# Eight small slots of 80, 64 and 48 tokens in an expert layer, both matrices stationary, and a written order on SyncE's queue

## The chip, the core and the metric

One core of a Trainium2 chip runs the whole program. The metric is the device time of one execution in microseconds (us). Engines are named as in the profile: PE (TensorE matmuls), PEld (TensorE weight loads), DVE (VectorE), ACT (ScalarE), POOL (GpSimd), SP (SyncE, which here only issues DMAs and loads registers). L809 is line 809 of the kernel before.

## The reference

Three layers in a row over 2304 tokens of 512 features. The change is in the last one, a mixture of eight experts of which each token takes two:

```python
def _moe2_ref(x, w_gate, w_noise, noise, w1, w2):
    logits = x @ w_gate
    noise_scale = np.log1p(np.exp(x @ w_noise))
    noisy_logits = logits + noise_scale * noise
    top2 = np.argpartition(-noisy_logits, 2, axis=1)[:, :2]
    ...
    for e in range(E):                      # 8 experts, D = 512, F = 1024
        for k in range(2):
            mask = top2[:, k] == e
            h = np.maximum(x[mask] @ w1[e], 0.0)
            out[mask] += top2_w[mask, k, None] * (h @ w2[e])
```

With the inputs of this case the experts 0 to 7 get 148, 573, 208, 22, 292, 1614, 1033 and 718 tokens (counted with the reference). Cut into blocks of 128, the last block of each holds 20, 61, 80, 22, 36, 78, 9 and 78 tokens.

## The kernel before

The first two layers, the gate and the sorting of tokens by expert take the first 450 us, and the change leaves them alone but for a few small DVE operations on eight numbers in the schedule. Then comes the expert stage. Tokens of one expert are dealt into **main blocks** of 128; the program has room for 36 of them, expert after expert (here 5, 6, 0, 7, 2, 1, 4). A last block of up to 64 tokens may go into one of five **small slots** of 64; the first five such experts by number get one (here 0, 1, 3, 4 and 6). `SEQ` is the fixed list of the 41 pieces: after the main blocks 8, 14, 20, 26 and 32 stands a small slot. What falls outside would run in a tail that is skipped here.

Values are split in fp16 high and low parts, and each product is three matmuls (high by high, low by high, high by low). A main block's first layer (`e1`, L809) is 24 matmuls with the block's tokens stationary and 512 weight columns moving, into the PSUM tile `ph`; ACT takes the relu (L816), DVE the low part (L817), and 16 DVE transposes of 32x32 squares (L830) bring `hr` to `ht`. The second layer (`e2`, L873) is again 24 matmuls of 512 columns into `py`; ACT scales it into `y` (L885) and POOL adds it into the output by an indirect DMA (L886). A small slot's `e1_small` (L843) has the weights stationary and 64 tokens moving, 96 matmuls, so that its output needs no transpose; its `e2_small` (L859) is 24 matmuls of 512 columns with 64 tokens stationary.

One step `t` of the loop puts on PE `e1(SEQ[t])` and then `e2(SEQ[t-3])`. What the other engines do is issued in the same loop:

- **Main weights.** `weights(i, half)` (L773) loads 2 MB, conditional on a flag: a block whose expert is that of the block before it moves nothing. Two halves of a buffer alternate by expert. W1(i+2), the first layer's weights, is issued after `e1(i)` and W2(j+2) after `e2(j)`. Before each W1, SP loads three registers. The first main blocks of the experts, whose loads are real, are here blocks 0, 13, 21, 22, 28, 30 and 34 of `SEQ`'s main blocks before the change (expert 3 has a small slot alone).
- **Small weights.** `weights_small` (L760) loads a slot's weights in four pieces of 1 MB, S1 high, S1 low, S2 high, S2 low, into a place of its own that all slots share. The four go out at the ends of the steps that stand in the loop below, counted from the slot before.
- **Tokens.** `prep` copies the block's token list (L782), gathers the tokens into `xr` by an indirect DMA on POOL's queue (L785), and issues on SP the DMA transpose `xt<-xr` (L792), all in the step six ahead of use.

```python
        for half, a, later in ((0, 0, 1), (0, 1, 2), (1, 0, 4), (1, 1, 5)):
            k = PARTS.get(t - later)
            if k is not None:
                weights_small(k, half, a)
        while preps and SEQ.index(preps[0]) <= t + AHEAD + 1 and (preps[0] < NBA or t >= PB):
            prep(preps.pop(0))
```

All SP issues are one in-order stream, and their DMAs one queue (q1 in the profile); POOL's are another (q0). `issue_after` and `LAST[...]` fix the order on an engine where they are used; transposes of later blocks are placed by the scheduler.

Of the kernel before, what the change touches and what calls it, by code (L numbers as in the profile page):

```python
# [22 lines left out]
P = 128  # L23
# [12 lines left out]
NSMALL = 5  # L36
NMAIN = 36
# [49 lines left out]
def body(ctx, tc, ins, out):  # L87
# [528 lines left out]
    def small(ni, nb, new, tt, ts, red):  # L616
        rest = ts(ni, 127, None, ALU.bitwise_and, dt=I32)
        few = ts(rest, 64.0, None, ALU.is_lt)
        some = tt([NE], few, ts(nb, 0.0, None, ALU.is_gt), ALU.mult)
        a, b = iota[:, None, :NE].to_broadcast([P, NE, NE]), iota[:, :NE, None].to_broadcast([P, NE, NE])  # L620
        less = tt([NE, NE], a, b, ALU.is_lt, F16)
        turn = red(tt([NE, NE], less, some[:, None, :].to_broadcast([P, NE, NE]), ALU.mult, F16))
        POS["turn"] = turn
        POS["small"] = tt([NE], some, ts(turn, float(NSMALL), None, ALU.is_lt), ALU.mult)
        POS["at"] = new(NE)
        nc.vector.scalar_tensor_tensor(out=POS["at"], in0=iota[:, :NE], scalar=float(NB), in1=nb, op0=ALU.mult, op1=ALU.add)
# [99 lines left out]
    SEQ = [i for m in range(NMAIN) for i in ((m, NBLK + m // 6 - 1) if m > 5 and m % 6 == 2 else (m,))]  # L726
    TI, XE, HT, PY, PT, REG, LIST, E = {}, {}, {}, {}, {}, {}, {}, {}
# [28 lines left out]
    def weights_small(i, half, a):  # L756
        with behind("sync"):
            if half + a == 0:
                WR[i] = nc.sync.value_load(entry(i, 2), min_val=0, max_val=NE - 1)
            w = nc.sync.dma_start(out=AR[half][:, 16384 + a * 4096:20480 + a * 4096],  # L760
                                  in_=wsc[ds(WR[i], 1), :, half, a].rearrange("o p f -> p (o f)"))
        (W1, W2)[half].setdefault(i, []).append(w)

    def weights(i, half):


        with behind("sync"):
            if half == 0:
# [5 lines left out]
                                  in_=wsc[ds(e, 1), :, half].rearrange("o p a f -> p (o a f)"), cond=(c == 1))  # L774
        (W1, W2)[half][i] = [w]

    def prep(i):
        ep, tab, at = E["ep"], LIST["a" if i < NBA else "b"][1], SEQ.index(i) if i in SEQ else i
# [9 lines left out]

        xt = E["ep2"].tile([P, 8, P], F16, name="xt2", bufs=2) if at > 5 and at % 3 == 0 else \
            ep.tile([P, 8, P], F16, name="xt", bufs=4)  # L790
        with behind("sync") if i < NBA else ExitStack():
            LAST["sync"] = nc.sync.dma_start_transpose(out=xt, in_=xr)  # L792
        TI[i], XE[i] = ti, xt
# [39 lines left out]
    def e1_small(i):  # L833
        xt, m = XE.pop(i), 0
        ph = E[bank(i)].tile([P, 512], F32, tag="ph", name="ph", bufs=2)
        ht = E["ep2"].tile([P, 2 * F2], F16, tag="ht", name="ht", bufs=5)
        M1[i] = []
        for f in range(8):
            with after() if f == 0 else ExitStack():
                for k in range(KC):  # L840
                    for a, b in ((0, 0), (1, 0), (0, 1)):
                        w = 16384 + b * 4096 + k * 1024 + f * 128
                        M1[i].append(nc.tensor.matmul(ph[:, f * HALF:(f + 1) * HALF], lhsT=AR[0][:, w:w + 128],  # L843
                                                      rhs=xt[:, a * 4 + k, :HALF], start=k + a + b == 0, stop=k == KC - 1 and b == 1))
# [34 lines left out]
    def combine(i):  # L879
# [3 lines left out]
        y, m = E["ep2"].tile([P, DM], F32, name="y", bufs=3), HALF if i >= NBLK else P  # L883
# [155 lines left out]
    LAG, AHEAD = 3, 5  # L1039
# [28 lines left out]
    for t in range(2, len(SEQ) + LAG):  # L1068
# [25 lines left out]
        for half, a, later in ((0, 0, 1), (0, 1, 2), (1, 0, 4), (1, 1, 5)):  # L1094
            k = PARTS.get(t - later)
            if k is not None:
                weights_small(k, half, a)
        while preps and SEQ.index(preps[0]) <= t + AHEAD + 1 and (preps[0] < NBA or t >= PB):
            prep(preps.pop(0))
            if preps and preps[0] == NBA + 2 and t == PB:  # L1100
                break
    weight_deps()
    with tc.If(nc.values_load(LIST["more"], min_val=0, max_val=1) > 0):  # L1103
        for i in range(NMAIN, NBLK):
# [3 lines left out]
            prep(i)  # L1108
            REG[i] = nc.tensor.value_load(entry(i, 1), min_val=0, max_val=1)
# [29 lines left out]
```

## Time and profile before

| | |
|---|---|
| runs | 889.49, 884.94, 885.11 us; median 885.11 us |
| profiled execution | 888.15 us; its span, first to last instruction, 886.4 us |
| mean granted TensorE clock | 0.988 |
| busy, share of the span | PE 97%, DVE 70%, PEld 50%, ACT 43%, POOL 32% |
| expert stage | from 450 us to the end at 886.4 us |

Times in the views below are counted from the span's first instruction. The span is 1.75 us shorter than the execution's own time.

### The profile page before, as it was taken

What the parts mean: (1) busy time and instruction counts of PE and PEld (TensorE: products, weight loads), DVE (VectorE), ACT (ScalarE), POOL (GpSimd) and SP (SyncE); (2) the same over time, 40 slices, a digit from 0 to 9 for tenths busy, and PEclk for the clock granted to TensorE, in tenths of its full rate; (3) what the DMA queues carried; (4) which work ended last, traced back from release to release, by engine and by line L of the source; (5) the groups of instructions that cost most, each with busy time, mean ns of one, the idle gap of its engine ahead of it and who ended that gap; (6) DMA issues with size and microseconds to landing.
All of it is one profiled execution on the core that took longest, in us unless ns stands there. A gap on an engine that the chain in (4) does not pass through costs nothing. (4 is left out here: it accounts for less than half of the span.)

```text
span 886.4 us, 19836 instructions
## 1 busy us (share of the span) xinstructions
PE 855.5 (97%) x6826; PEld 445.5 (50%) x6826; DVE 621.6 (70%) x1299; ACT 384.8 (43%) x599; POOL 287.6 (32%) x276
## 2 busy tenths in 40 slices
PE   6799999999999999999999999999999999989995
PEld 6455555555555555555544444445445445434542
DVE  5999978686786777554459785775885886758552
ACT  3989767676665786574421121221212111211110
POOL 3876224242612412422305323222233222312212
PEclk9899999999999999999999999999999999989998
DMA  9977599899799898962776986787559998697442
GB/s 335 383 292 210 189 269 326 286 308 327 248 328 327 278 314 311 317 218 52 225 185 132 179 162 147 215 203 194 155 125 301 215 236 228 165 296 186 166 120 40
DMA packets 143908, 203.72 MB, mean 230 GB/s; under 512 B 79872, under 2 KB 90368, under 8 KB 139456
## 3 DMA queue, kind: packets, MB, share of 16 engines
q1 hardware_dynamic: 133632, 181.34, 65.7%
q0 software_dynamic: 10176, 21.05, 12.3%
q8 instruction: 63, 1.03, 0.5%
q14 instruction: 37, 0.30, 0.1%
HBM read 245.67 MB, written 53.55 MB: 338 GB/s over the span
## 5 line engine op out<-in xcount | busy, mean ns | idle before, releaser
L830 DVE STREAM_TRANSPOSE ht<-hr 32x256 f32<-32x256 f32 x528 | 230.1, 436 | 10.2 <-DVE hr L817 0.5
L321 PE MATMUL pg<-x,wi 128*128 128x384 f16 x1152 | 203.8, 327 | 1.4 <-POOL x L310 0.8
L809 PE MATMUL ph<-w,xt 128*128 x864 | 195.3, 383 | 5.2 <-DMA w<-wsc 4.5
L363 PE MATMUL p<-w,g 128*128 128x512 f16 x864 | 199.7, 379 | 0.0
L873 PE MATMUL py<-w,ht 128*128 x864 | 192.1, 379 | 0.2 <-DMA w<-wsc 0.2
L886 POOL DMA_INDIRECT out_dram<-y,ti x41 | 64.3, 1568 | 278.0 <-ACT y L885 225.1
L321 PEld LDWEIGHTS <-wi 128*128 128x128 f16 x1152 | 110.8, 98 | 82.2 <-issue 3.2
L809 PEld LDWEIGHTS <-xt 128*128 128x128 f16 x864 | 84.8, 99 | 110.2 <-issue 11.5
L873 PEld LDWEIGHTS <-ht 128*128 128x128 f16 x864 | 84.2, 98 | 101.2 <-DMA w<-wsc 0.6
L363 PEld LDWEIGHTS <-g 128*128 128x128 f16 x864 | 83.4, 98 | 91.9 <-issue 0.2
L817 DVE SCALAR_TENSOR_TENSOR hr<-ph,hr 128x512 f16<-128x512 f32 x72 | 52.4, 728 | 107.4 <-ACT hr L816 106.5
L816 ACT ACTIVATE hr<-ph 128x512 f16<-128x512 f32 x72 | 52.6, 732 | 141.1 <-PE ph L809 141.1
L885 ACT ACTIVATE y<-py,ti 128x512 f32<-128x512 f32 (+1 forms) x41 | 28.2, 687 | 187.2 <-PE py L873 163.8
L400 DVE SCALAR_TENSOR_TENSOR w<-w 128x1024 f16<-128x1024 f32 x64 | 90.9, 1446 | 16.1 <-ACT w L396 15.7
L332 ACT ACTIVATE r<-pg 128x384 f32<-128x384 f32 x96 | 46.9, 488 | 102.3 <-PE pg L321 97.9
L342 DVE SCALAR_TENSOR_TENSOR r<-a,r 128x768 f32<-128x768 f32 x48 | 49.1, 1022 | 56.6 <-ACT a L338 49.2
L350 POOL TENSOR_TENSOR g<-r,g 128x768 f16<-128x768 f32 x27 | 46.9, 1737 | 95.6 <-ACT g L142 51.2
L595 POOL DMA_INDIRECT table<-tb,pos x36 | 44.4, 1233 | 75.1 <-DVE scb L649 23.3
L396 ACT ACTIVATE w<-w 128x1024 f16<-128x1024 f32 x64 | 65.6, 1054 | 1.4 <-DMA w<-in_moe_w_dram 1.4
L785 POOL DMA_INDIRECT xr<-X,ti x41 | 43.3, 1055 | 23.4 <-DMA xt<-xr 11.6
L333 ACT ACTIVATE a<-pg 128x384 f32<-128x384 f32 x96 | 46.6, 485 | 0.0
L338 ACT ACTIVATE a<-a 128x768 f32<-128x768 f32 x48 | 40.6, 845 | 1.5
(152 smaller groups left out, 698.2 us busy)
## 6 DMA issues: line engine op xcount, KB each, us to landing
w<-wsc SPq DMA_DIRECT2D x68, 2048.0 KB
w<-in_moe_w_dram SPq DMA_DIRECT2D x64, 512.0 KB
wsc<-w SPq DMA_DIRECT2D x64, 512.0 KB
w<-wsc SPq DMA_DIRECT2D x20, 1024.0 KB
kv<-in_kv_dram SPq DMA_DIRECT2D x18, 512.0 KB
qk<-in_qk_dram SPq DMA_DIRECT2D x18, 512.0 KB
w<-in_moe_w_out_dram SPq DMA_DIRECT2D x8, 1024.0 KB
w<-in_moe_w_in_dram SPq DMA_DIRECT2D x7, 1024.0 KB
```

What stands on the lines that cost most here:

```text
L321: nc.tensor.matmul(pg, lhsT=wi[:, a, k, f * P:(f + 1) * P], rhs=x[:, b, k, :], start=n == 0, stop=n == 11)
L332: LAST["relu"] = nc.scalar.activation(PG["r", i][:, j], pg, AF.Relu, scale=S_G / SX)
L342: nc.vector.scalar_tensor_tensor(out=r, in0=PG.pop(("a", i)), scalar=S_G, in1=r, op0=ALU.mult, op1=ALU.add)
L363: LAST["p2"] = nc.tensor.matmul(PG[t, j], lhsT=g[:, a, f % 2, j * P:(j + 1) * P], rhs=wo[b][:, f, :], start=f == 0 and a + b == 0, stop=f ...
L396: nc.scalar.activation(h[:, 0], WL[n], AF.Copy, scale=(S_W1, S_W2)[(n // 4) % 2])
L400: nc.vector.scalar_tensor_tensor(out=h[:, 1], in0=t, scalar=(S_W1, S_W2)[(n // 4) % 2], in1=h[:, 0], op0=ALU.mult, op1=ALU.subtract)
L809: M1[i].append(nc.tensor.matmul(ph, lhsT=xt[:, a * 4 + k, :], rhs=AR[0][:, ds(r * 8192 + (b * 4096 + k * 1024 + n * 512), 512)], start=m = ...
L816: LAST["act"] = nc.scalar.activation(hi, ph, AF.Relu)
L817: nc.vector.scalar_tensor_tensor(out=lo, in0=ph, scalar=0.0, in1=hi, op0=ALU.max, op1=ALU.subtract)
L830: nc.vector.transpose(dst[32 * f:32 * f + 32, :, t], src[32 * t:32 * t + 32, :, f])
L873: M2[i].append(nc.tensor.matmul(py, lhsT=ht[:, c, :, a], rhs=AR[1][:, ds(r * 8192 + (b * 4096 + c * 512), 512)], start=len(M2[i]) == 0, st ...
L886: LAST["pool"] = nc.gpsimd.indirect_dma_start(out=out[:, :], out_offset=bass.IndirectOffsetOnAxis(ap=ti[:m, 1:2], axis=0), in_=y[:m, :], i ...
```

## The change

There are eight small slots instead of five, of 80, 80, 80, 64, 48, 48, 48 and 48 tokens. Experts are ranked by the size of their last block, the largest first, and a last block goes into the slot of its rank if it fits. With this case's inputs all eight fit (80, 78, 78, 61, 36, 22, 20 and 9 tokens), one of them exactly. The program has room for 33 main blocks, so `SEQ` still has 41 pieces; the slots stand after the main blocks 7, 10, 13, ..., 28, which is every fourth piece from `SEQ[8]` on. The first main blocks of experts are now 0, 12, 20, 21, 26, 27 and 31.

`e1_small` (L868 after the change) moves as many tokens as the slot has, into two `ph` tiles with a relu and a low part each. `e2_small` (L887) has the weights stationary too: 96 matmuls of the slot's tokens, and 8 or 12 DVE transposes out of PSUM into `y` (L895). ACT scales `y` in place. S2's pieces go out a step earlier than before. A transpose on SP is no longer issued with its gather but in the step four ahead of use (`turn`), and every SP issue of the loop is tied to the one before it.

```diff
--- before.py
+++ after.py
@@ -33,8 +33,9 @@
-NSMALL = 5
-NMAIN = 36
+CAPS = (80, 80, 80, 64, 48, 48, 48, 48)
+NSMALL = len(CAPS)
+NMAIN = 33
...
-        few = ts(rest, 64.0, None, ALU.is_lt)
+        few = ts(rest, float(max(CAPS)), None, ALU.is_lt)
...
+        key = new(NE)
+        nc.vector.scalar_tensor_tensor(out=key, in0=rest, scalar=8.0, in1=iota[:, :NE], op0=ALU.mult, op1=ALU.add)
+        more = tt([NE, NE], a, b, ALU.is_gt, F16)
+        turn = red(tt([NE, NE], more, some[:, None, :].to_broadcast([P, NE, NE]), ALU.mult, F16))
...
-        POS["small"] = tt([NE], some, ts(turn, float(NSMALL), None, ALU.is_lt), ALU.mult)
+        POS["small"] = tt([NE], some, tt([NE], cap, rest, ALU.is_gt), ALU.mult)
...
-    SEQ = [i for m in range(NMAIN) for i in ((m, NBLK + m // 6 - 1) if m > 5 and m % 6 == 2 else (m,))]
+    AT = [7 + 3 * n for n in range(NSMALL)]
+    SEQ = [i for m in range(NMAIN) for i in ((m, NBLK + AT.index(m)) if m in AT else (m,))]
...
                 WR[i] = nc.sync.value_load(entry(i, 2), min_val=0, max_val=NE - 1)
             w = nc.sync.dma_start(out=AR[half][:, 16384 + a * 4096:20480 + a * 4096],
                                   in_=wsc[ds(WR[i], 1), :, half, a].rearrange("o p f -> p (o f)"))
+        LAST["sync"] = w
         (W1, W2)[half].setdefault(i, []).append(w)
...
+        TI[i], XR[i] = ti, xr
+        if i < NBA:
+            turn(i)
+
+    def turn(i):
+        ep, xr, at = E["ep"], XR.pop(i), SEQ.index(i) if i in SEQ else i
         xt = E["ep2"].tile([P, 8, P], F16, name="xt2", bufs=2) if at > 5 and at % 3 == 0 else \
             ep.tile([P, 8, P], F16, name="xt", bufs=4)
-        with behind("sync") if i < NBA else ExitStack():
+        with behind("sync"):
             LAST["sync"] = nc.sync.dma_start_transpose(out=xt, in_=xr)
-        TI[i], XE[i] = ti, xt
+        XE[i] = xt
...
     def e1_small(i):
-        xt, m = XE.pop(i), 0
-        ph = E[bank(i)].tile([P, 512], F32, tag="ph", name="ph", bufs=2)
+        xt, m, rows = XE.pop(i), 0, CAPS[i - NBLK]
         ht = E["ep2"].tile([P, 2 * F2], F16, tag="ht", name="ht", bufs=5)
+        hs = HT[i] = ht[:, :16 * rows].rearrange("p (a c t) -> p a c t", a=2, c=8)
         M1[i] = []
-        for f in range(8):
-            with after() if f == 0 else ExitStack():
-                for k in range(KC):
+        for n in range(2):
+            ph = E[bank(i)].tile([P, 512], F32, tag="ph", name="ph", bufs=2)
+            for f in range(4):
+                with after() if f == 0 else ExitStack():
+                    for k in range(KC):
+                        for a, b in ((0, 0), (1, 0), (0, 1)):
+                            w = 16384 + b * 4096 + k * 1024 + (n * 4 + f) * 128
+                            M1[i].append(nc.tensor.matmul(ph[:, f * rows:(f + 1) * rows], lhsT=AR[0][:, w:w + 128],
+                                                          rhs=xt[:, a * 4 + k, :rows], start=k + a + b == 0,
+                                                          stop=k == KC - 1 and b == 1))
+            LAST["pe"] = M1[i][-1]
+            hi, lo = (hs[:, a, n * 4:n * 4 + 4].rearrange("p c t -> p (c t)") for a in range(2))
+            LAST["act"] = nc.scalar.activation(hi, ph[:, :4 * rows], AF.Relu)
+            nc.vector.scalar_tensor_tensor(out=lo, in0=ph[:, :4 * rows], scalar=0.0, in1=hi, op0=ALU.max, op1=ALU.subtract)
+
+    def e2_small(i):
+        hs, rows = HT.pop(i), CAPS[i - NBLK]
+        wide = -(-rows // 32) * 32
+        full = hs.rearrange("p a c t -> p a (c t)")
+        py = E[bank(i)].tile([P, 4, P], F32, tag="py", name="py", bufs=2)
+        M2[i] = []
+        for g in range(4):
+            with after() if g == 0 else ExitStack():
+                for c in range(8):
                     for a, b in ((0, 0), (1, 0), (0, 1)):
-                        w = 16384 + b * 4096 + k * 1024 + f * 128
-                        M1[i].append(nc.tensor.matmul(ph[:, f * HALF:(f + 1) * HALF], lhsT=AR[0][:, w:w + 128],
-                                                      rhs=xt[:, a * 4 + k, :HALF], start=k + a + b == 0, stop=k == KC - 1 and b == 1))
-        LAST["pe"] = M1[i][-1]
-        hi, lo = (ht[:, a * 512:(a + 1) * 512] for a in range(2))
-        LAST["act"] = nc.scalar.activation(hi, ph, AF.Relu)
-        nc.vector.scalar_tensor_tensor(out=lo, in0=ph, scalar=0.0, in1=hi, op0=ALU.max, op1=ALU.subtract)
-        HT[i] = ht[:, :1024].rearrange("p (a c t) -> p c t a", a=2, c=8)
-
-    def e2_small(i):
-        ht = HT.pop(i)
-        py = E[bank(i)].tile([P, DM], F32, tag="py", name="py", bufs=2)
-        M2[i] = []
-        for c in range(8):
-            with after() if c == 0 else ExitStack():
-                for a, b in ((0, 0), (1, 0), (0, 1)):
-                    w = 16384 + b * 4096 + c * 512
-                    M2[i].append(nc.tensor.matmul(py[:HALF], lhsT=ht[:, c, :, a], rhs=AR[1][:, w:w + 512],
-                                                  start=len(M2[i]) == 0, stop=len(M2[i]) == 23))
+                        w, n = 16384 + b * 4096 + c * 512 + g * 128, wide if c + a + b == 0 else rows
+                        M2[i].append(nc.tensor.matmul(py[:, g, :n], lhsT=AR[1][:, w:w + 128],
+                                                      rhs=full[:, a, c * rows:c * rows + n],
+                                                      start=c + a + b == 0, stop=c == 7 and b == 1))
         LAST["pe"] = M2[i][-1]
-        PY[i] = py
+        y = PY[i] = E["ep2"].tile([P, DM], F32, name="y", bufs=3)
+        v = y.rearrange("p (g f) -> p g f", g=4)
+        for f in range(4):
+            for t in range(wide // 32):
+                nc.vector.transpose(v[32 * t:32 * t + 32, :, 32 * f:32 * f + 32], py[32 * f:32 * f + 32, :, 32 * t:32 * t + 32])
 
...
-        y, m = E["ep2"].tile([P, DM], F32, name="y", bufs=3), HALF if i >= NBLK else P
+        y, m = (py, CAPS[i - NBLK]) if i >= NBLK else (E["ep2"].tile([P, DM], F32, name="y", bufs=3), P)
         with behind("act"):
             nc.scalar.activation(y[:m], py[:m], AF.Copy, scale=ti.bitcast(F32)[:m, 3:4])
...
-    LAG, AHEAD = 3, 5
+    LAG, AHEAD, LATE = 3, 5, 4
+
+    def turns(last):
+        for i in [i for i in XR if SEQ.index(i) <= last]:
+            turn(i)
...
-        for half, a, later in ((0, 0, 1), (0, 1, 2), (1, 0, 4), (1, 1, 5)):
+        for half, a, later in ((0, 0, 1), (0, 1, 2), (1, 0, 3), (1, 1, 4)):
             k = PARTS.get(t - later)
             if k is not None:
                 weights_small(k, half, a)
+        turns(t + LATE)
         while preps and SEQ.index(preps[0]) <= t + AHEAD + 1 and (preps[0] < NBA or t >= PB):
             prep(preps.pop(0))
+            turns(t + LATE)
```

On SP, around the loads of the first block of expert 1 before the change (block 30; `w_84` is the first layer's buffer, `w_85` the second's, L773 main weights, L760 a small slot's, the TENSOR_LOADs the three registers):

```order
L760 DMA w_84<-wsc 128x4096 [waits DMAHW6_49]
L792 DMA_TRANSPOSE xt<-xr 128x8x128 [waits DMAHW7_49,DMASW2_49]
L769 TENSOR_LOAD bib
...
L773 DMA w_84<-wsc 128x8192 [waits DMAHW0_49,PE_49]
L792 DMA_TRANSPOSE xt_10333<-xr 128x8x128 [waits DMAHW1_49,DMASW4_49]
L769 TENSOR_LOAD bib
...
L773 DMA w_84<-wsc 128x8192 [waits DMAHW2_49,PE_49]
...
L773 DMA w_85<-wsc 128x8192 [waits DMAHW3_49,PE_49]
L760 ISA
L760 DMA w_85<-wsc 128x4096 [waits DMAHW4_49]
```

After the change, SP two steps ahead of the last slot (L789 is main weights, W1(29) and W2(27); L775 the slot's S1 low; L815 the transpose):

```order
L789 DMA w_84<-wsc 128x8192 [waits DMAHW6_49,PE_49]
...
L789 DMA w_85<-wsc 128x8192 [waits DMAHW7_49,PE_49]
L775 ISA
L775 DMA w_84<-wsc 128x4096 [waits DMAHW0_49]
L815 DMA_TRANSPOSE xt<-xr 128x8x128 [waits DMAHW1_49,DMASW2_49]
```

The transpose that waits for a gather (DMASW) stood ahead of the next block's register loads and of W1; it now stands behind the loads of its step, and its gather was issued two steps earlier. S1 low stands right behind a W2, as it did before.

On DVE, around a small slot before (L817 low part, L830 transposes, L848 the slot's low part):

```order
L817 SCALAR_TENSOR_TENSOR hr<-ph,hr 128x512 x2
L830 STREAM_TRANSPOSE ht<-hr 32x8x32 x16
L848 SCALAR_TENSOR_TENSOR ht<-ph,ht 128x512
L817 SCALAR_TENSOR_TENSOR hr<-ph,hr 128x512 x2
L830 STREAM_TRANSPOSE ht<-hr 32x8x32 x16
```

And after, at a slot of 80 tokens (L840, L853 and L874 are those three, L895 the new transposes out of `py`):

```order
L840 SCALAR_TENSOR_TENSOR hr<-ph,hr 128x512 x2
L853 STREAM_TRANSPOSE ht<-hr 32x8x32 x16
L895 STREAM_TRANSPOSE y<-py 32x4x32 x12
L874 SCALAR_TENSOR_TENSOR ht<-ph,ht 128x320 x2
L840 SCALAR_TENSOR_TENSOR hr<-ph,hr 128x512 x2
L853 STREAM_TRANSPOSE ht<-hr 32x8x32 x16
```

Behind a main block's 16 transposes, 12 more follow for the slot before, ahead of the low part of the next slot.

## Rows read from the trace of the kernel before

**Rows 1.** The page's first part: busy us, share of the span, instructions.

```profile
PE 855.5 (97%) x6826; PEld 445.5 (50%) x6826; DVE 621.6 (70%) x1299; ACT 384.8 (43%) x599; POOL 287.6 (32%) x276
```

**Rows 2.** PE's groups: line, engine, operation, tiles, count | busy, mean ns | idle before.

```profile
L809 PE MATMUL ph<-w,xt 128*128 x864 | 195.3, 383 | 5.2 <-DMA w<-wsc 4.5 <-DVE hr L817 0.6
L873 PE MATMUL py<-w,ht 128*128 x864 | 192.1, 379 | 0.2 <-DMA w<-wsc 0.2
L859 PE MATMUL py<-w,ht 128*64 128x512 f16 x120 | 26.8, 380 | 0.0
L843 PE MATMUL ph<-xt,w 128*128 128x64 f16 x480 | 15.5, 193 | 0.4
L843 PEld LDWEIGHTS <-w 128*128 128x128 f16 x480 | 14.9, 98 | 2.0 <-issue 0.7
```

**Rows 3.** PE's timeline, 650 to 668: start, length, instructions.

```profile
651.93 5.34 PE L809 MATMUL ph<-w,xt 128*128 x24
657.11 5.34 PE L873 MATMUL py<-w,ht 128*128 x24
662.29 5.34 PE L809 MATMUL ph<-w,xt 128*128 x24
```

**Rows 4.** PE's timeline around small slots: 696 to 727, then 737 to 753.

```profile
706.91 5.37 PE L859 MATMUL py<-w,ht 128*64 128x512 f16 x24
712.21 5.35 PE L809 MATMUL ph<-w,xt 128*128 x24
...
743.30 3.15 PE L843 MATMUL ph<-xt,w 128*128 128x64 f16 x96
746.29 5.34 PE L873 MATMUL py<-w,ht 128*128 x24
```

**Rows 5.** PE's timeline, 455 to 460, and 200 to 207: matmuls of 16 and 384 columns.

```profile
457.91 1.05 PE L501 MATMUL lg<-wg,x2t 128*128 128x16 f16 x36
458.82 1.46 PE L809 MATMUL ph<-w,xt 128*128 x6
...
203.85 2.12 PE L321 MATMUL pg<-x,wi 128*128 128x384 f16 x12
205.82 1.46 PE L363 MATMUL p<-w,g 128*128 128x512 f16 x6
```

**Rows 6.** The waits: engine, tile, line, releaser: total us, times, longest.

```profile
PE ph L809 <- DMA w<-wsc: 4.5, 2, 4.0
SPq L792 <- DMA xr<-X,ti: 156.5, 33, 10.3
```

**Rows 7.** PE's timeline, 752 to 800.

```profile
761.83 5.34 PE L809 MATMUL ph<-w,xt 128*128 x24
767.01 5.34 PE L873 MATMUL py<-w,ht 128*128 x24
...
777.46 5.37 PE L859 MATMUL py<-w,ht 128*64 128x512 f16 x24
786.85 8.24 PE L809 MATMUL ph<-w,xt 128*128 x24 [4.02 <-DMA w<-wsc]
794.93 5.34 PE L873 MATMUL py<-w,ht 128*128 x24
```

**Rows 8.** SP's timeline, 760 to 800.

```profile
764.74 0.36 SPq L760 DMA_DIRECT2D w<-wsc  x1
772.94 1.25 SPq L792 DMA_TRANSPOSE xt<-xr  x1
777.66 1.15 SPq L773 DMA_DIRECT2D w<-wsc  x2
779.02 0.35 SPq L760 DMA_DIRECT2D w<-wsc  x1
```

**Rows 9.** Windows: stretch, length, busy us by engine, granted clock, DMA share, GB/s.

```profile
667.00:677.00 10.00, 9.89 (x129) 5.99 (x128) 8.14 (x18) 2.03 (x3) 2.49 (x3) 1.00 1.05 369
698.00:725.00 27.00, 27.00 (x126) 12.29 (x125) 22.66 (x50) 5.04 (x7) 5.54 (x6) 1.00 1.11 291
785.90:792.80 6.90, 5.95 (x15) 2.20 (x16) 0.44 (x1) 0.59 (x1) 1.04 (x1) 0.51 0.99 378
```

**Rows 10.** DMA traffic, 698 to 725: packets, bytes, then by queue, with share of 16 engines.

```profile
DMA packets 3016, 7.86 MB, mean 291 GB/s; under 512 B 2176, under 2 KB 2176, under 8 KB 2501
...
q1 hardware_dynamic: 2567, 6.79, 93.3%
q0 software_dynamic: 446, 1.02, 17.2%
```

**Rows 11.** The page's fifth part: DVE's groups.

```profile
L830 DVE STREAM_TRANSPOSE ht<-hr 32x256 f32<-32x256 f32 x528 | 230.1, 436 | 10.2 <-DVE hr L817 0.5
L817 DVE SCALAR_TENSOR_TENSOR hr<-ph,hr 128x512 f16<-128x512 f32 x72 | 52.4, 728 | 107.4 <-ACT hr L816 106.5
```

More of the change, by code (lines that the diff above doesn't have):

```diff
@@ L617, in small @@
         rest = ts(ni, 127, None, ALU.bitwise_and, dt=I32)
-        few = ts(rest, 64.0, None, ALU.is_lt)
+        few = ts(rest, float(max(CAPS)), None, ALU.is_lt)
         some = tt([NE], few, ts(nb, 0.0, None, ALU.is_gt), ALU.mult)
-        a, b = iota[:, None, :NE].to_broadcast([P, NE, NE]), iota[:, :NE, None].to_broadcast([P, NE, NE])
-        less = tt([NE, NE], a, b, ALU.is_lt, F16)
-        turn = red(tt([NE, NE], less, some[:, None, :].to_broadcast([P, NE, NE]), ALU.mult, F16))
+        key = new(NE)
+        nc.vector.scalar_tensor_tensor(out=key, in0=rest, scalar=8.0, in1=iota[:, :NE], op0=ALU.mult, op1=ALU.add)
+        a, b = key[:, None, :].to_broadcast([P, NE, NE]), key[:, :, None].to_broadcast([P, NE, NE])
+        more = tt([NE, NE], a, b, ALU.is_gt, F16)
+        turn = red(tt([NE, NE], more, some[:, None, :].to_broadcast([P, NE, NE]), ALU.mult, F16))
+        cap = None
+        for m in range(len(CAPS) - 1, -1, -1):
+            if m == len(CAPS) - 1 or CAPS[m] != CAPS[m + 1]:
+                left = ts(turn, float(m), None, ALU.is_le)
+                if m == len(CAPS) - 1:
+                    cap = ts(left, float(CAPS[m]), None, ALU.mult)
+                else:
+                    wider = cap
+                    cap = new(NE)
+                    nc.vector.scalar_tensor_tensor(out=cap, in0=left, scalar=float(CAPS[m] - CAPS[m + 1]), in1=wider,
+                                                   op0=ALU.mult, op1=ALU.add)
         POS["turn"] = turn
-        POS["small"] = tt([NE], some, ts(turn, float(NSMALL), None, ALU.is_lt), ALU.mult)
+        POS["small"] = tt([NE], some, tt([NE], cap, rest, ALU.is_gt), ALU.mult)
         POS["at"] = new(NE)
@@ L723, in schedule @@
         return bi, tab
-    SEQ = [i for m in range(NMAIN) for i in ((m, NBLK + m // 6 - 1) if m > 5 and m % 6 == 2 else (m,))]
-    TI, XE, HT, PY, PT, REG, LIST, E = {}, {}, {}, {}, {}, {}, {}, {}
+    AT = [7 + 3 * n for n in range(NSMALL)]
+    SEQ = [i for m in range(NMAIN) for i in ((m, NBLK + AT.index(m)) if m in AT else (m,))]
+    TI, XR, XE, HT, PY, PT, REG, LIST, E = {}, {}, {}, {}, {}, {}, {}, {}, {}
     M1, M2, W1, W2, WR = {}, {}, {}, {}, {}
@@ L774, in weights @@
                                   in_=wsc[ds(e, 1), :, half].rearrange("o p a f -> p (o a f)"), cond=(c == 1))
+        LAST["sync"] = w
         (W1, W2)[half][i] = [w]
     def prep(i):
-        ep, tab, at = E["ep"], LIST["a" if i < NBA else "b"][1], SEQ.index(i) if i in SEQ else i
+        ep, tab = E["ep"], LIST["a" if i < NBA else "b"][1]
         with behind("pool"):
@@ L1108, in body @@
             prep(i)
+            turn(i)
             REG[i] = nc.tensor.value_load(entry(i, 1), min_val=0, max_val=1)
```

## The prediction

> **What bounds the kernel now.** I read the page's first part, then PE's groups, its timeline, the waits, and last SP's timeline with the DMA windows. PE is busy 97% of the span [rows 1], so the stage is worth what its matmuls are worth, plus what PE waits. In the expert stage two main groups hold 387 us (195.3 + 192.1), the small slots 42 us (26.8 + 15.5) [rows 2]. The timeline shows the beat: a new piece every 5.18 us, from 651.93 to 657.11 to 662.29 [rows 3], whatever stands in between; DVE, ACT and POOL follow. So fewer matmuls show in the time one for one, as long as nothing that PE waits for comes later than now.
>
> PE waits little: 4.5 us in all for main weights, of which 4.0 in one place [rows 6]. That place is the first block of expert 1: the e2 of a slot starts at 777.46 and the next e1 only at 786.85, after 4.02 us of idleness, and this e1 then takes 8.24 us where the next piece takes 5.34 [rows 7]. The granted clock there is 0.51, the lower of the two levels (1.2 of 2.4 GHz) [rows 9]: an idle PE is paid for twice, 4.02 + 2.90 us.
>
> The load was late because SP issued it late. The buffer was free when e1(28) ended at about 767.0 (the e2 behind it starts there [rows 7]); the load went out at 777.66, behind a transpose at 772.94, 8.2 us after SP's issue before it [rows 8]. SP spends 156.5 us, in 33 places, waiting for gathers in front of transposes [rows 6].
>
> **The matmuls, step by step.** A main block costs two pieces, 2 x 5.18 = 10.36 us [rows 3]; three fewer save 31.1. An old slot costs 5.30 for e2 (706.91 to 712.21) and 2.99 for e1 (743.30 to 746.29) [rows 4], 8.29 together; five save 41.4.
>
> New slots have 192 matmuls each. At 64 columns one takes 2.99 / 96 = 31.1 ns [rows 4]. No row has 80 or 48. At 16 columns it is (458.82 - 457.91) / 36 = 25.3 ns, at 384 it is (205.82 - 203.85) / 12 = 164 ns, 0.43 a column [rows 5]. For 80 I take 31.1 plus 16 columns at 0.43, 37.9 ns; the lower bound is 80 times 0.43, 34.4. For 48 the bounds are 25.3 and 31.1; I take 27, nearer the small end, since 48 columns at 0.43 would be 20.6. Then three slots of 80 cost 7.28 each, the one of 64 costs 5.97, four of 48 cost 5.18 each: 21.8 + 6.0 + 20.7 = 48.5 us (bounds 45.2 and 51.7). Matmuls in all: 48.5 - 31.1 - 41.4 = **-24.0** (-27.3 to -20.8).
>
> On this a page speaks against the change. The row of e1_small shows one matmul each 31.1 ns although each has a weight load of its own, whose mean is 98 ns [rows 2, 4]. The Trainium skill ("TensorE: Matmul & The Clock Gate", section "Back-to-back issue gap") gives about 81 ns as the sustained spacing of load and matmul pairs at 128 columns; by it the new slots would take up to 8 x 192 x 81 ns = 124 us. The trace disagrees for 64 columns, and the sum goes by the trace; what is left of the doubt is the fourth case below.
>
> **The order on SP.** With the transposes two steps further from their gathers and behind the loads of their step, W1 of expert 1's first block goes out when its buffer is free, some 24 us ahead of use (a slot and two main blocks lie between). The two waits for main weights and the slow e1 go: 4.5 + 2.9 = **-7.4** [rows 6, 7]. Nothing of it is gained if the transposes come late themselves, but they are due four steps, some 38 us, later.
>
> **The new wait.** It is S1 low, the second piece of a slot's first matrix. It is issued at the end of the step two ahead of e1_small, behind the W2 of that step; PE has then one main e1 (5.18) and the e2 of the slot before (2.6 to 3.6), together 7.8 to 8.8 us. Before, five steps lay between. The first matmul of e1_small needs all of S1, and everything on PE stands behind it in order.
>
> Where the W2 ahead moves nothing, 1.05 MB at the lowest rate of rows 9 takes 3.6 us: no wait. But slots come every three main blocks, so W2(6 + 3k) stands there for slot k (k from 0), and it is real where that is an expert's first block: 12, 21 and 27, for k = 2, 5 and 7. What is then to land, at 291 to 369 GB/s (two stretches with the DMA engines full [rows 9]) and 1.0 us to issue (1.15 and 0.35 for such calls [rows 8]):
>
> - k = 2: 2.10 + 1.05 MB, with 0.5 MB of gather and scatter beside it (1.02 MB of POOL's queue in 27 us [rows 10]): 3.65 MB, 9.9 to 12.5 us. Minus 8.8, plus 1.0: a stall of 2.1 to 4.7.
> - k = 5 and 7: the step before also has a real W2 (20 and 26, single-block experts follow each other) with S1 high and a transpose behind it. From there it is 6.55 MB and 1.05 of POOL's, 20.6 to 26.1 us, against 10.36 + 7.8 = 18.1 us of PE: stalls of 3.5 to 9.0 each. Just this sequence of five transfers ran before, too, in 698 to 725: 6.79 MB on SP's queue in 27 us at 291 GB/s [rows 9, 10]. I take 7.0.
>
> Middle values: 3.0 + 7.0 + 7.0 = 17. Each also puts PE on the lower clock, 2.9 at the one stall that shows it (4.02 us); I take 2.9 for the long two and 2.2 for the short, 8 in all (bounds 0, if the clock came back at once, and 8.7). **+25** (9 to 31). The Trainium skill's ceiling is another: "DMA: Bandwidth & Descriptors", section "Where 436 GB/s comes from", names about 435 GB/s; at that rate the stalls would be 0.6 and 0.4 us, which is the second case below; no stretch of rows 9 reaches it.
>
> **What costs nothing.** The 8 or 12 new DVE transposes have half the columns of the 436 ns ones [rows 11]; between 0.07 us (nothing but a start) and 0.44 us each, 12 take 0.8 to 5.3. A period of four steps is about 38 us and has 3 x (16 x 0.436 + 2 x 0.73) = 25.3 us of DVE, so there is room; they delay the slot's low part and scatter, not PE, whose e2 is three steps away. Without this cover a slot would pay up to 5.3. ACT's second relu (0.3) goes the same way. Schedule: ten or so small DVE operations, about 1 us, while PE has e1 of blocks 0 to 2; uncovered it is +1. The last three pieces and the scatter at the end are as before. S2 goes out a step earlier but has the steps to e2 as cover. Each is bounded by 0 and +1 to the end.
>
> **Sum.** -24.0 - 7.4 + 25 = -6.4, plus 1 for the uncovered small ones: about -5 from 886.4, a span of 881. Execution adds 1.75. This profiled run lay 3.0 us above the median; from the median of 885.1 it makes **880**.
>
> **The cases.**
>
> 1. *Three stalls eat most of it* (0.57): 872 to 889, middle 880. For: the full DMA engines in rows 9 and 10. Against: the same engines moved 369 GB/s over 10 us.
> 2. *No stall worth the name* (0.18): waits of 0 to 6 us in all, -24.0 - 7.4 + 3 = -28, so 854 to 863. For: the traffic of POOL's queue may lie outside these stretches. Against: a stall of nothing needs 7.6 MB in 17.1 us, 444 GB/s, against 291 in the same sequence.
> 3. *The loads saturate and the stalls pass the gain* (0.21): **slower**. The break-even is where stalls and clock make 31.4 us. The three stalls sum to (3.65 + 2 x 7.6) MB over the rate, minus 8.8 + 2 x 18.1, plus 3; with 8.7 for the clock, that is 31.4 at 291 GB/s, just the rate of rows 9. At 260 it is 39 us; and k = 4 and 6, where a real W1 (20 and 26) shares the step with S1 low, may then wait some 4 each with the clock: +16 at most, 890 to 901, middle 893.
> 4. *The spacing is set by weight loads after all* (0.02): e2_small's 96 matmuls take 98 ns each instead of about 31, 8 x 96 x 67 ns = 51 us more: 930. Against: rows 4, where e1_small runs at 31.
> 5. *The change doesn't do what it says* (0.02): the block of exactly 80 doesn't fit and goes to the tail, a block by itself behind the end: 4.2 MB at 300 GB/s, two pieces and a gather, 14 + 10.4 + some 8: 33 us, 913.
>
> Faster by over 0.5% (a measurement here can tell no less), under 880.7: half of case 1 and all of case 2, 0.47. Within 0.5%, up to 889.5: the rest of case 1, 0.28. Slower: 0.25. The range leaves out a tenth on each side: 857 to 894; case 1 alone has 872 to 889.
>
> **What would show it.** In the trace after: L868 with 96 matmuls in 3.6, 3.0 and 2.6 us for 80, 64 and 48, and L887 the same; three waits of L868 for DMA weights, at the third, sixth and eighth slot, the second and third about 7 us, and a lower granted clock behind them; no wait of L832 for weights; SP's transposes with hardly a wait for gathers. I am wrong if L868 has no such waits (case 2), if they are more than 25 us in all or stand at other slots (case 3), or if L887 takes over 5 us.

## The result

The changed kernel takes 893.13 us (median of 5 runs, 890.36 to 893.32), the kernel before 886.27 (5 runs, 884.94 to 889.49): a ratio of 1.0068, interval 1.0044 to 1.0092. (Here and below the ratio with its 95% interval is the one on record; it is not the quotient of the two medians.) The kernel is slower by 0.7%, where 880 and "faster" were forecast. The time lies in the range, near its upper end; the sign is wrong.

The page of the changed kernel, first part, beside [rows 1]: PE is busy 20 us less, and the span is 891.3 us, 4.9 more.

```profile
PE 835.1 (94%) x7618; PEld 458.1 (51%) x7618; DVE 622.0 (70%) x1339; ACT 381.5 (43%) x604; POOL 289.6 (32%) x276
```

So the matmuls were saved, and more than that went to idleness. The waits of the changed kernel name the place, beside [rows 6] (L868 is `e1_small`):

```profile
SPq L815 <- DMA xr<-X,ti: 10.3, 4, 8.0
PE ph L868 <- DMA w<-wsc: 14.2, 3, 7.3
PE ph L868 <- issue: 11.9, 2, 6.2
```

SP's 156.5 us of waiting for gathers are 10.3 now, and the 4.0 us wait of a main block is gone; in their place the slots wait 26.1 us. PE's timeline shows each, and what the slots' matmuls cost (L887 is the slots' second layer, L906 a main block's):

```profile
557.39 3.63 PE L887 MATMUL py<-ht,w 128*128 128x96 f16 x96
560.85 3.61 PE L868 MATMUL ph<-xt,w 128*128 128x80 f16 x96
564.29 5.35 PE L906 MATMUL py<-w,ht 128*128 x24
...
603.37 5.65 PE L868 MATMUL ph<-xt,w 128*128 128x80 f16 x96 [4.37 <-DMA w<-wsc]
...
686.64 3.71 PE L868 MATMUL ph<-xt,w 128*128 128x48 f16 x96 [6.23 <-issue]
690.19 5.34 PE L906 MATMUL py<-w,ht 128*128 x24
...
729.52 4.00 PE L868 MATMUL ph<-xt,w 128*128 128x48 f16 x96 [5.65 <-issue]
...
769.90 2.57 PE L868 MATMUL ph<-xt,w 128*128 128x48 f16 x96 [2.50 <-DMA w<-wsc]
...
813.30 3.58 PE L868 MATMUL ph<-xt,w 128*128 128x48 f16 x96 [7.31 <-DMA w<-wsc]
...
847.80 2.60 PE L887 MATMUL py<-ht,w 128*128 128x64 f16 x96
850.24 5.34 PE L906 MATMUL py<-w,ht 128*128 x24
```

Starts give the prices: e2 of a slot of 80 takes 560.85 - 557.39 = 3.46 us, one of 48 takes 850.24 - 847.80 = 2.44. Slots 2, 4, 5, 6 and 7, counted from 0, wait 4.37, 6.23, 5.65, 2.50 and 7.31 us. Behind four of them the e1 takes 1.0 to 2.1 us longer than without a wait (690.19 - 686.64 = 3.55 where 2.41 is usual, and so on): the granted clock in these four is 0.50 to 0.60, in the e1 behind the wait of 2.50 it is 1.00.

For two of the waits, those of slots 4 and 5, the profile names "issue": it saw no event that ended them. SP's timeline of the changed kernel, here around slot 4, shows that S1 low goes out as short a time ahead of use there as at the other three, 6.9 to 8.0 us (L789 main weights, L775 a slot's, L815 the transpose):

```profile
669.02 3.38 SPq L789 DMA_DIRECT2D w<-wsc  x2
672.61 0.36 SPq L775 DMA_DIRECT2D w<-wsc  x1
673.07 6.07 SPq L815 DMA_TRANSPOSE xt<-xr  x1
681.34 1.06 SPq L789 DMA_DIRECT2D w<-wsc  x1
682.66 0.82 SPq L775 DMA_DIRECT2D w<-wsc  x1
683.59 10.69 SPq L815 DMA_TRANSPOSE xt<-xr  x1
```

S1 low of slot 4 goes out at 672.61, some 7.8 us before PE wants it at 680.4. Right ahead of it, at 669.02, stands W1 of block 20, an expert's first block. What the queues do meanwhile, by the DMA traffic from 669 to 673 and by the window behind it (its last two columns are DMA share and GB/s):

```profile
DMA packets 880, 0.34 MB, mean 84 GB/s; under 512 B 835, under 2 KB 835, under 8 KB 875
```

```profile
673.00:687.00 14.00, 7.77 (x127) 5.22 (x126) 11.96 (x28) 1.63 (x3) 2.84 (x3) 0.85 1.05 312
```

For 4 us, with W1's 2 MB issued, nearly all packets are small ones, as a transpose has them (839 of the 880 are on SP's queue); then come 14 us at 312 GB/s, 4.4 MB, enough for W1 and S1 low with the transposes and the gather beside them.

The end is late too. DVE, ACT and POOL of the changed kernel, same timeline, after the e2 of the last slot (847.80 to 850.24):

```profile
849.62 7.18 DVE L853 STREAM_TRANSPOSE ht<-hr 32x256 f32<-32x256 f32 x16
856.83 2.58 DVE L895 STREAM_TRANSPOSE y<-py 32x128 f32<-32x128 f32 x8
...
859.59 0.72 ACT L918 ACTIVATE y<-y,ti 48x512 f32<-48x512 f32 x1 [10.84 <-DVE y L895]
860.22 0.67 ACT L918 ACTIVATE y<-py,ti 128x512 f32<-128x512 f32 x1
...
860.58 1.35 POOL L919 DMA_INDIRECT out_dram<-y,ti  x1 [15.12 <-ACT y L918]
...
883.18 1.54 POOL L919 DMA_INDIRECT out_dram<-y,ti  x1 [4.01 <-DMA out_dram<-y,ti]
```

The slot's transposes wait for 16 others, ACT waits 10.84 us for them with the next block's `y` behind it, the slot's scatter goes out at 860.58, and four more follow, on the average 5.65 us apart, to 883.18; for the last one the profile names the scatter before it as what it waited for. In the kernel before, the last scatter is 5.0 us earlier:

```profile
878.17 1.55 POOL L886 DMA_INDIRECT out_dram<-y,ti  x1 [4.32 <-DMA out_dram<-y,ti]
```

The sum of the two profiled spans goes from the first matmul of the expert stage to the last 72, and on to the end (first before, then after):

```profile
450.14 7.93 PE L809 MATMUL ph<-w,xt 128*128 x36
860.11 15.70 PE L873 MATMUL py<-w,ht 128*128 x72
...
452.87 7.93 PE L832 MATMUL ph<-w,xt 128*128 x36
860.60 15.70 PE L906 MATMUL py<-w,ht 128*128 x72
```

Its terms: first matmul of the expert stage 450.14 before, 452.87 now, +2.7; waits in the stage 5.4 before, 26.8 now, +21.4; slow matmuls behind waits 2.9 before, 6.0 now, +3.1; from the start of the last 72 matmuls (860.11 and 860.60) to the end 26.3 before, 30.7 now, +4.4; what is left of the 4.9 is the matmuls, -26.7. The first term is hardly the change's: the kernel before with one edit in the expert stage alone (below) starts that stage at 452.6, and the ten other profiles below lie between 452.3 and 454.4. Why the one profile of the kernel before starts it earliest of all is not known.

### The profile page after: what moved, and what is told of

It is laid out like the page before. It is cut to its first block, busy times and chain, and to the rows that moved or that the text cites. A ratio compares the mean times of both kernels' runs of the same rounds, so it can differ in the third digit from the quotient of the medians.

```text
span 891.3 us, 21301 instructions
## 1 busy us (share of the span) xinstructions
PE 835.1 (94%) x7618; PEld 458.1 (51%) x7618; DVE 622.0 (70%) x1339; ACT 381.5 (43%) x604; POOL 289.6 (32%) x276
## 5 line engine op out<-in xcount | busy, mean ns | idle before, releaser
L853 DVE STREAM_TRANSPOSE ht<-hr 32x256 f32<-32x256 f32 x480 | 209.2, 436 | 8.6
L906 PE MATMUL py<-w,ht 128*128 x792 | 176.5, 379 | 0.5 <-issue 0.5
L832 PE MATMUL ph<-w,xt 128*128 x792 | 176.2, 379 | 0.3 <-DMA w<-wsc 0.3
L832 PEld LDWEIGHTS <-xt 128*128 128x128 f16 x792 | 77.4, 98 | 93.4 <-issue 0.6
L906 PEld LDWEIGHTS <-ht 128*128 128x128 f16 x792 | 77.0, 98 | 92.4 <-issue 1.6
L840 DVE SCALAR_TENSOR_TENSOR hr<-ph,hr 128x512 f16<-128x512 f32 x66 | 47.9, 728 | 95.0 <-ACT hr L839 92.7
L839 ACT ACTIVATE hr<-ph 128x512 f16<-128x512 f32 x66 | 48.0, 732 | 114.8 <-PE ph L832 114.8
L918 ACT ACTIVATE y<-py,ti 128x512 f32<-128x512 f32 x33 | 22.6, 686 | 131.0 <-PE py L906 130.9
L868 PE MATMUL ph<-xt,w 128*128 128x48 f16 (+2 forms) x768 | 29.7, 207 | 26.1 <-DMA w<-wsc 14.2
```

The costliest lines, as they stand in the source:

```text
L832: M1[i].append(nc.tensor.matmul(ph, lhsT=xt[:, a * 4 + k, :], rhs=AR[0][:, ds(r * 8192 + (b * 4096 + k * 1024 + n * 512), 512)], start=m = ...
L853: nc.vector.transpose(dst[32 * f:32 * f + 32, :, t], src[32 * t:32 * t + 32, :, f])
L906: M2[i].append(nc.tensor.matmul(py, lhsT=ht[:, c, :, a], rhs=AR[1][:, ds(r * 8192 + (b * 4096 + c * 512), 512)], start=len(M2[i]) == 0, st ...
```

## The experiments

Each was timed against the kernel before on the same chip; the ratio is what compares, since the chips differ from run to run.

**S1 low one step earlier** (`s1_low_early`, and a second time `s1_early_again`).

```diff
-        for half, a, later in ((0, 0, 1), (0, 1, 2), (1, 0, 3), (1, 1, 4)):
+        for half, a, later in ((0, 0, 1), (0, 1, 1), (1, 0, 3), (1, 1, 4)):
```

> The changed kernel with one number changed: S1 low is issued in the same step as S1 high, one step (10.4 us) earlier. Theory A, S1 low comes late only because it is issued two steps ahead behind a real W1 or W2: the five waits of e1_small (26.1 us in all) fall to under 4 us, and the slow matmuls behind them (6.0 us) with them; 893.1 - 22 to 32, so 861 to 871. Theory B, the queue as a whole is full in these stretches, and what is put earlier only makes the next load late: the waits move to other loads (W1, W2, S2 or the next slot), their sum stays above 15 us, and the time is 882 or more.

Measured: 875.05 us against 889.27, ratio 0.9868 (0.9819 to 0.9917). What is left of the slots' waits is named "issue":

```profile
PE ph L868 <- issue: 5.7, 5, 2.1
```

Theory A holds in the main: one number takes 20 of 26 us of waits away, and no other load of PE's comes late. The same bytes fit the queue; they stood in the wrong place. But 5.7 us are left where under 4 were expected, and the median is 4 us above the 861 to 871 of theory A. By PE's timeline 2.9 of the 5.7 us lie ahead of a slot's first matmul (slots 5 and 7) and 2.8 in the middle of a slot.

> s1_low_early once more, beside the two next ones on one chip; its runs were 870 to 879. If what varies is whether a slot's S1 lands in time, this profile has waits at slots of 3 to 12 us that follow the time (about 868 + waits - 5.7 for the span); if it is the first two layers that vary, the first matmul of the expert stage moves with the time and the waits stay at 5 to 6.

Measured: 871.58 against 886.37, ratio 0.9838 (0.9790 to 0.9886). Waits at slots 8.9 us, the longest 4.7 at slot 6, with a span of 870.3; the stage starts at 453.50, and at 454.38 in the first. So the waits move with the time, as the first case of the expectation has it, but its cause is not borne out: 6.4 of the 8.9 us lie in the middle of a slot, the 4.7 after 24 of slot 6's 96 matmuls, and S1 low is used from the third matmul on.

```profile
754.30 3.04 PE L868 MATMUL ph<-xt,w 128*128 128x48 f16 x72 [4.68 <-issue]
```

That leaves at most 2.5 us to S1 landing late. These are two profiles; the runs of up to 879 us have none.

**The slots one block later** (`slots_one_block_later`).

```diff
-    AT = [7 + 3 * n for n in range(NSMALL)]
+    AT = [8 + 3 * n for n in range(NSMALL)]
```

> The changed kernel with the slots after main blocks 8, 11, ..., 29 in place of 7, 10, ..., 28. S1 low then never stands behind a real W2; a real W1 is in its step for slots 1, 4 and 6 (W1 of blocks 12, 21 and 27). Theory A (S1 low waits for the 2 MB that is ahead of it in its own step): no wait at slots 2, 5 and 7, waits of 2 to 6 us at 1, 4 and 6 (as now at 4 and 6, where the load ahead is a W1), 8 to 16 us in all, 876 to 884. Theory B (the queue is full as a whole): 20 us or more of waits in all, at these or other loads, 887 or more.

Measured: 883.39 against 889.27, ratio 0.9931 (0.9898 to 0.9963). PE's timeline:

```profile
576.67 5.18 PE L868 MATMUL ph<-xt,w 128*128 128x80 f16 x96 [4.30 <-issue]
622.03 1.62 PE L868 MATMUL ph<-xt,w 128*128 128x80 f16 x22 [2.85 <-issue]
698.51 3.30 PE L868 MATMUL ph<-xt,w 128*128 128x48 f16 x96 [3.07 <-DMA w<-wsc]
739.30 3.18 PE L868 MATMUL ph<-xt,w 128*128 128x48 f16 x96 [3.25 <-issue]
782.34 3.57 PE L868 MATMUL ph<-xt,w 128*128 128x48 f16 x96 [5.07 <-issue]
821.24 3.21 PE L868 MATMUL ph<-xt,w 128*128 128x48 f16 x96 [1.81 <-DMA w<-wsc]
```

Slot 1, which had no wait, now has W1 of block 12 in its step and waits: a real W1 does what a real W2 does. Slots 1, 4 and 6 wait 4.30, 3.07 and 5.07, within the 2 to 6 of theory A, and the time is in its range. But slots 5 and 7, with no real load in that step, still wait 3.25 and 1.81, where none was expected. (Slot 2's 2.85 us come after 74 of its 96 matmuls and are not a wait for S1.) At slots 5 and 7 SP was late itself: the issue of a transpose held it for 7.88 and 8.65 us (from 721.36 and 803.08), and S1 low went out at 732.53 and 815.08, 3.5 and 4.4 us before PE wanted it. The waits come to 20.4 us in all, where theory A had 8 to 16 and theory B 20 or more; they are those of the longest of the ten runs (877 to 887). So a real load in S1 low's own step is enough for a wait, but not the only way to one. Read with the run above: wherever an expert begins, SP and its queue are some microseconds behind for more than one step, so that a load issued 4 to 8 us ahead of use is late, and one issued 14 to 18 us ahead, as there, is in time or 1 to 2 us late.

**The written order by itself**, once added to the kernel before (`before_with_written_order`) and once taken out of the changed one (`changed_without_written_order`). The comments are added here.

```diff
+        LAST["sync"] = w            # in weights and weights_small
...
-        with behind("sync") if i < NBA else ExitStack():
+        with behind("sync"):        # in turn, split from prep
...
+        turns(t + LATE)             # LATE = 4
```

> The kernel before with only the written order on SP (transposes four steps ahead and behind the loads of their step, every issue tied to the one before), with its five slots, places and small loads as they were. Theory E, as the prediction had it: the wait of 4.0 us at the first block of expert 1, the 0.5 us one and the slow e1 (2.9) go, 886.3 - 7.4 = 879. Theory F, a transpose still stands in the queue ahead of every load, and loads behind it start when it is through: the waits for main weights stay at 3 us or more or come at other places, 884 to 888.

Measured: 881.19 against 889.27, ratio 0.9923 (0.9897 to 0.9948). The first block of expert 1 follows without a gap, beside [rows 7] (L867 the slot's e2, L817 the block's e1):

```profile
779.06 5.37 PE L867 MATMUL py<-w,ht 128*64 128x512 f16 x24
784.36 5.35 PE L817 MATMUL ph<-w,xt 128*128 x24
```

Theory E: from its later start (452.6) the stage is 7.7 us shorter, 7.4 were expected.

> The changed kernel with SP's order as before: each transpose issued in the step of its gather, and the issues not tied. Theory E, the written order is worth some 7 us here too: SP waits for gathers again (over 100 us in all, against 10), loads go out later, the waits of PE for weights grow from 26 to 30 us or more, among them one at the first block of expert 1 or 4, and the time is 897 to 903. Theory F, the loads are late because of the bytes in the queue and not because of SP's waits: waits of 24 to 28 us as now, 891 to 895.

Measured: 924.81 against 888.17, ratio 1.0403 (1.0356 to 1.0451). The wait for gathers is back on SP (155.6 us in 32 places), and slots wait 54 us in all; four of seven:

```profile
701.31 3.91 PE L865 MATMUL ph<-xt,w 128*128 128x48 f16 x96 [12.52 <-DMA w<-wsc]
748.41 4.00 PE L865 MATMUL ph<-xt,w 128*128 128x48 f16 x96 [9.67 <-DVE y L892]
794.26 3.65 PE L865 MATMUL ph<-xt,w 128*128 128x48 f16 x96 [8.13 <-issue]
844.29 4.02 PE L865 MATMUL ph<-xt,w 128*128 128x48 f16 x96 [12.86 <-DMA w<-wsc]
```

The sign is that of theory E, the size four times what was expected, some 30 us: with slots every fourth step it is not one late W1 that stands behind an SP that waits, but most slots' S1. (That it is S1 is read from three of the names; 19.2 us are named "issue", and 9.7 go to a DVE transpose.) The written order is what keeps the eight slots from costing 4%.

**The end** (`last_slot_second_layer_early`).

```diff
-        early = t == len(SEQ) - 1
+        early = t == len(SEQ) - 1 or j == NBLK + NSMALL - 1
```

> The changed kernel with the second layer of the last slot ahead of the first layer in its step, and so its DVE transposes ahead of a main block's 16. Theory C, the end is 4.4 us later than before because the last slot's y waits for these 16 transposes (scatter issued at 860.6 where its e2 ended at 850.2) and each scatter waits for the one before: from the last matmul to the end it takes 10.6 us as before, not 15.0, and the time falls by 3.5 to 5, to about 889. Theory D, the last blocks' own y sets the end: no change within 1 us, 892 to 894.

Measured: 887.75 against 889.27, ratio 0.9999 (0.9974 to 1.0025), where the changed kernel had 1.0068. In its timeline the last 72 matmuls start at 862.24 and the last scatter goes out at 880.51:

```profile
862.24 15.70 PE L906 MATMUL py<-w,ht 128*128 x72
...
880.51 1.54 POOL L919 DMA_INDIRECT out_dram<-y,ti  x1 [4.10 <-DMA out_dram<-y,ti]
```

From there to the end it is 888.6 - 862.2 = 26.4 us, as before the change and 4.3 less than after: theory C. The five waits are as large as ever (26.7).

**Both together** (`s1_early_last_slot_early`).

> s1_low_early and last_slot_second_layer_early together. If the two causes are independent the times add: from the last matmul to the end 10.6 us in place of 15.4, 4 to 5 less than s1_low_early, so about 870.5. Rival: with the matmuls 23 us earlier the scatters before the last are still under way and the end gains less than 2: 873 or more.

Measured: 866.24 against 888.17, ratio 0.9748 (0.9704 to 0.9791). The last 72 matmuls start at 837.15, the span ends at 863.2: 26.1 us. The causes are independent: the end gains 4.6 us with the stage as long as in `s1_low_early` within 1.5. The time is below what was expected; that was reckoned from the 875 of the first timing of `s1_low_early`, and the second gave 871.58.

**Tokens stationary in the second layer again**, on top of `s1_low_early` (`s1_early_tokens_stationary`).

```diff
-                        M2[i].append(nc.tensor.matmul(py[:, g, :n], lhsT=AR[1][:, w:w + 128], ...
+                    M2[i].append(nc.tensor.matmul(py[:rows], lhsT=hs[:, a, c, :], rhs=AR[1][:, w:w + 512], ...
```

> The kernel s1_low_early with the second layer of the slots as before the change: 24 matmuls of 512 columns with the tokens stationary, no transposes out of PSUM. Theory: each such e2 takes 5.30 us in place of 2.44 (48 tokens), 2.7 (64) and 3.46 (80), so 8 x 5.30 - 4 x 2.44 - 2.7 - 3 x 3.46 = 19.6 us more PE time; less 4.4 at the end, where no y waits for transposes, and up to 4 of the waits named issue, if those are PE's supply of instructions: 875 + 11 to 16, 886 to 891. Rival: weights-stationary matmuls run no faster in the whole, since what they save comes back as waits: 878 or less.

Measured: 878.88 against 888.17, ratio 0.9880 (0.9836 to 0.9923). One e2 of a slot of 48 is again a full piece:

```profile
717.09 5.36 PE L884 MATMUL py<-w,ht 128*48 128x512 f16 x24
```

From the stage's first matmul to the last 72 it takes 398.5 us against 383.3 in `s1_low_early`, +15.2 with 4.0 less of waits, so 19.2 of matmuls where 19.6 were expected. The end is 4.4 shorter, as it should be without transposes. In the profiles that makes 15.2 - 4.4 = 10.8 us, the low end of the 11 to 16 expected. The time misses its expectation (886 to 891) and lies near the rival's 878: it is 3.8 and 7.3 us above the two medians of `s1_low_early` (875.05 and 871.58, on other chips), and by the ratios only 0.1 and 0.4% slower. So as the change was made, much of what the weights-stationary form saves on PE is lost again at the end and in waits. Against the pair with the end mended (866.24, same chip) it is worth 12.6 us.

**The second layer of every slot early** (`s1_early_all_slots_early`, again as `all_slots_early_again`, and with S1 high a step earlier still as `all_slots_early_s1_high_earlier`).

```diff
-        early = t == len(SEQ) - 1
+        early = t == len(SEQ) - 1 or j is not None and j >= NBLK
...
-        for half, a, later in ((0, 0, 1), (0, 1, 1), (1, 0, 3), (1, 1, 4)):
+        for half, a, later in ((0, 0, 0), (0, 1, 1), (1, 0, 3), (1, 1, 4)):   # the third only
```

> s1_low_early with the second layer of every slot ahead of the first layer of the main block in its step; before, the e2 of one slot and the e1 of the next, 384 short instructions in 5 us, stood back to back on PE. Theory G, the 5.7 us of waits left in s1_low_early (named issue, some in the middle of an e1_small) are PE waiting for its instructions behind the loads in the DMA engines: with a main block's 5.2 us between them they fall under 2.5, and with the 4.4 at the end the time is about 867. Theory H, they are S1 landing late: they stay at 5 to 6, and the time is that of s1_early_last_slot_early within 1.5.

Measured: 862.10 against 888.17, ratio 0.9677 (0.9633 to 0.9722). Its profiled execution was its longest, 871.53, with 5.93 us at slot 7. Neither theory fits: the slots' waits stay at 7.5 us in this profile, and the median is 4 us below `s1_early_last_slot_early` on the same chip.

> s1_early_all_slots_early once more: four of its runs were 859 to 863 and the profiled one 871.5, with a wait of 5.9 at slot 7 where S1 stood behind a real W2 and a transpose that took 8 us. Theory G: most runs have under 3 us of waits at slots, 858 to 864. Theory H: the waits belong to it, 866 to 872.

Measured: 859.89 against 886.37, ratio 0.9720 (0.9672 to 0.9769). That is theory G's range. This profile, of the shortest of its four runs (span 855.3), has no wait at any slot's first layer; all that PE waits in the stage for its expert matmuls is

```profile
PE ph L832 <- DMA w<-wsc: 0.6, 1, 0.6
PE py L887 <- issue: 0.4, 1, 0.4
PE py L906 <- issue: 0.2, 1, 0.2
```

> all_slots_early with S1 high issued another step earlier, in the step of the e1 of the slot before, so that S1 high and S1 low stand in steps of their own. If slot 7's S1 is tight because both pieces stand behind one real W2, the waits for S1 fall under 2 us and the slow runs of 870 go: 857 to 862. If the queue is full as a whole there, S1 low alone behind W2 is as late, within 1.5 of all_slots_early_again.

Measured: 858.67 against 886.37, ratio 0.9690 (0.9644 to 0.9736), waits at the slots' first layers 2.4 us, and one of 2.0 at a main block instead, in the profile of its longest run. It cannot be told from `all_slots_early_again`. Either is some 3% faster than the kernel before, and some 3.5% faster than the change as it was made.

## Why the prediction was wrong, step by step

- **Matmuls, -24.0 forecast, -26.7 measured.** Right, and within the bounds. 48 columns run at 2.44 us / 96 = 25 ns, at the lower bound; 80 at 36 ns. The case that weight loads set the spacing fell: the new matmuls, each with a weight load of its own, run at 25 to 36 ns. The Trainium skill's 81 ns ("TensorE: Matmul & The Clock Gate", section "Back-to-back issue gap") is for 128 columns, a width that the slots do not have.
- **The order on SP, -7.4 forecast, -7.1 measured** (4.5 + 2.9 before; 0.3 of waits for main weights is left). Right, shown by the kernel before with this part alone. That the same order was worth some 30 us in the changed kernel had not been seen.
- **The stalls at slots 2, 5 and 7, 17 forecast, 17.3 measured.** Right in place and sum, and each within its bounds (4.37, 5.65 and 7.31, where 3.0, 7.0 and 7.0 were taken). The cause was named too narrowly: with no W2 in the step, slots 5 and 7 still waited (`slots_one_block_later`).
- **This step failed: "Where the W2 ahead moves nothing ... no wait".** Slots 4 and 6 wait 6.23 and 2.50, with 1.1 of slow matmuls: 9.9 us that the sum put at nothing and only case 3 mentioned. The 3.6 us for 1.05 MB took a free queue and the lowest rate of [rows 9], 291 GB/s; 84 GB/s were seen for 4 us in their place. The sum looked for a real W2 in S1 low's own step and passed over the real W1 (blocks 20 and 26) that SP issues a few microseconds ahead in that step. Moved slots moved such a wait to slot 1, and one more step of lead took away 20 of the 26 us.
- **This step failed too: "The last three pieces and the scatter at the end are as before".** The prediction saw that new DVE transposes would delay a slot's scatter, and did not ask who waits for the last one: ACT with the next `y` behind it, and a chain of scatters some 5.65 us apart. 4.4 us, shown by moving one e2.
- **Clock, 8 forecast for the three stalls, 4.8 measured there** (6.0 with slot 4's 1.1, which stands in the 9.9). A stall of 4 to 7 us ahead of a slot cost 1.0 to 2.1 us, less than the 2.9 ahead of a main block.
- **What costs nothing.** The DVE transposes took 2.58 / 8 = 0.32 us each, within 0.07 to 0.44, and in the changed kernel no wait of PE is put down to them; the end is told above.
- **The sum.** A span of 881 was forecast, 891.3 was measured, 10.3 more. The two failed steps are 9.9 + 4.4 = 14.3; the later start of the stage adds 2.7; matmuls (-2.7), clock (-3.2) and the uncovered small ones (-1) take some of it back. Without the two steps the span would have been 877, on the side that was forecast; with S1 low earlier and the end mended the same change gives 866.
- **Case 3 had this time as its middle, 893, and that is partly luck.** Its signs came: over 25 us of waits, and some at slots 4 and 6. But it had the three stalls and their clock at 31.4 us or more, and they were 22.1; it had up to 16 for slots 4 and 6, and they were 9.9; and the 4.4 of the end were in no case.

What stays open: the waits of 0.2 to 4.7 us that are left inside `e1_small`. They fall at fixed places of the program: in three runs slot 4 stops after 86 of its 96 matmuls (`s1_low_early`, `s1_early_last_slot_early`, `s1_early_again`):

```profile
680.11 0.41 PE L868 MATMUL ph<-xt,w 128*128 128x48 f16 x10 [2.14 <-issue]
```

```profile
677.67 0.56 PE L868 MATMUL ph<-xt,w 128*128 128x48 f16 x10 [1.95 <-issue]
```

```profile
678.25 0.41 PE L868 MATMUL ph<-xt,w 128*128 128x48 f16 x10 [1.50 <-issue]
```

In the same three slot 5 stops after 55. No weight is awaited in the middle of a slot. That PE's instructions come late there, past the full DMA engines, fits the fixed place, and so does `s1_early_tokens_stationary`: with 24 matmuls in place of 96 in each e2 of a slot, no such wait is over 0.4 us. It was argued and not shown. The Trainium skill ("Runtime: NRT & Kernel Launch", section "Instruction fetch mechanics") has the instruction memory refilled by DMA in blocks and calls the cost mostly hidden; if it is that, 384 short instructions in 5 us are where it shows. Nor was it settled why the 5.93 us at slot 7 came in one profiled execution and not in the next.

## What to carry to other kernels

Before a load is costed as hidden, add up all real transfers that its queue issues in the two or three steps ahead, of every kind, against the time to its use; an average rate says nothing of the microseconds where an expert begins. Ask also what holds the engine that issues the load. One more step of lead turned a loss of 0.7% into a gain of 1.3 to 1.6%. When work moves to an engine that is not the bound, follow its last item to the end of the program, since there nothing hides it. And the parts of a change can be worth something else together than alone: the order saved 0.8% by itself, and some 3% beside the eight slots, which cost 4% without it.

## What was not expected of the hardware

- Issued loads can stand still: 0.34 MB in 669 to 673, 84 GB/s, against 291 to 369 in [rows 9], with W1 issued at 669.02 behind a transpose, and a gather (POOL, 667.37) under way. The lower bound that the prediction took from the kernel before was too high for such a stretch; whether the transpose or the gather holds the loads was not tried.
- A transpose holds SP itself: its issue took 1.25 us in [rows 8] and 10.69 us at 683.59 in the changed kernel, and the loads behind it are issued that much later.
- The first two layers, the same in all kernels, ended up to 4 us apart in the profiles (450.1 to 454.4); a difference of up to 0.5% between two single executions can come from there.
